# Cross-network kernel: loads of the first rows, bias vectors and first weights on other queues, and the prologue's small matmuls in one tile shape

## The chip, the core and the metric

The kernel runs on one core of a Trainium2 chip. A core has TensorE for matrix products, VectorE, ScalarE and GpSimd for elementwise work, SyncE for issuing transfers, and 16 DMA engines [...]. TensorE reads from SBUF and writes to PSUM, which here is eight banks of 512 fp32 columns in 128 partitions. The metric is device time in microseconds, the median of several runs; lower is better.

## The reference

The computation is a cross network of six layers on a batch of 4096 rows with 416 features:

```python
B, F, D, L = 4096, 26, 16, 6          # 26 * 16 = 416 features
x = x0                                 # (4096, 416), bf16
for l in range(L):
    x = x0 * (x @ ws[l] + bs[l]) + x   # ws (6, 416, 416), bs (6, 416)
```

The kernel rewrites this. With x = x0 * y, each layer is y <- y + x @ W + b. So PSUM accumulates the sums of x @ W over the layers, and the biases enter as running sums over the layers, computed once at the start.

## The kernel before

**Tiling.** The batch is cut into four superblocks of 1024 rows, each of two halves of 512 rows. Features lie along the partitions, in three chunks of 128 (384 features) and a tail of 32. A layer on a superblock is a set of matmuls with 512 moving columns. TensorE is split into four column tiles of 32: each chunk of outputs is four matmuls `128*32`, which run side by side (`tile_mm`, L265 records them). The tail features use row tiles of 32 (L393, L409). After each group, VectorE forms (PSUM + bias sum) * x0 (L537), and ScalarE and GpSimd do the same for the tail.

**The prologue.** Before the first layer can start, TensorE needs three things. The first is the bias sums `cb_sb`, the second the first rows transposed (`x0T_sb`), the third the first weights W0 (`w_sb`). TensorE's program there is, in order:

- 40 warm-up matmuls on a constant (L130), which need no data;
- `bias_sums()`: 16 matmuls of 6 columns, which multiply `bsa_sb` (a row of ones over the six bias rows) with `u_sb` (a triangle of ones);
- `fill(1)`: one round of four more matmuls on the constant;
- twelve transposes (L312) of the first 512 rows, in the order of `IN_ORDER`: three column chunks of the row pair `h = 1`, then three of `h = 0`. VectorE (L512) and ScalarE (L561) copy the results to `x0T_sb`;
- the first layer, n = 0, whose first chunk waits for W0 and for these copies. In its middle stand `tail_inputs()` and `third_input()`, which bring the tail features and the third row pair in feature order by products with the identity matrix.

Rows 768 to 1023 come by a transposing DMA that SyncE issues when the row pair 0 has landed (L158).

**The queues.** SyncE and ScalarE each issue transfers in program order. Row pair i is `xin_sb[:, 2*i:2*i+2, :]`, 208 KB, with semaphore `s_xin[i]`. SyncE issues the biases, pair 0, pair 2. ScalarE issues pair 1, W0 (312 KB), the tail columns of the last rows (`xtl_sb`), two pieces of `wt_sb`, and then begins its computing work, which opens with a load of its activation table. GpSimd issues the rest of layer 0's tail weights and waits for a cleared `wc_sb` first (`s_zero`).

**Semaphores that the change touches.** `s_bs` (biases loaded), `s_zero` (VectorE's memsets done), `s_set` (GpSimd's identity and triangle made), `s_xin[0..2]` (row pairs loaded), `s_w[0]` (W0 loaded), `s_inT` (a chunk transposed), `s_inD` and `s_inA` (copied by VectorE, by ScalarE).

Of the kernel before, what the change touches and what calls it, by code (L numbers as in the profile page):

```python
# [8 lines left out]
ACTF = mybir.ActivationFunctionType  # L9


def bass_standalone__dcn_v2_cross__recsys_kernel(
# [6 lines left out]
    B, D = x0.shape  # L19
    L = ws.shape[0]  # L20
# [7 lines left out]
    G = SB // 4  # L28
# [4 lines left out]
    with ExitStack() as es:  # L33
        def sb(name, shape, dt=BF16):
            return es.enter_context(nc.sbuf_tensor(name, shape, dt))
# [4 lines left out]
        xin_sb = sb("xin_sb", [128, 6, D])  # L40
        xtl_sb = sb("xtl_sb", [128, 2, DR])
        x4_sb = sb("x4_sb", [128, NS - 1, SB])
        x0T_sb = sb("x0T_sb", [128, NC, B])
# [10 lines left out]
        o_sb = sb("o_sb", [128, NJ, D])  # L54
        ident = sb("ident", [128, 128])
        ones_sb = sb("ones_sb", [128, 256])
        bsa_sb = sb("bsa_sb", [L + 1, D])
        u_sb = sb("u_sb", [L + 1, L])
        cb_sb = sb("cb_sb", [128, NC + 1, L], FP32)
        cq_sb = sb("cq_sb", [128, NC + 2], FP32)  # L60
        ps = es.enter_context(nc.psum_tensor("ps", [128, 8, 512], FP32))
        psT = ps.bitcast(BF16)
# [4 lines left out]
        s_ones, s_set, s_zero = sem("s_ones"), sem("s_set"), sem("s_zero")  # L67
        s_wtp, s_wc = sem("s_wtp"), [sem("s_wc%d" % i) for i in range(2)]
        s_bs, s_cbp, s_cb = sem("s_bs"), sem("s_cbp"), sem("s_cb")
        s_xin = [sem("s_xin%d" % i) for i in range(3)]  # L70
# [4 lines left out]
        s_inT, s_inD, s_inA = sem("s_inT"), sem("s_inD"), sem("s_inA")  # L75
# [12 lines left out]
        x0_w = x0.rearrange("(g p r) d -> p g r d", p=128, r=2)  # L88
# [9 lines left out]
        IN_BANKS = ((3, 4, 6), (0, 5, 7))  # L98
        IN_ORDER = ((1, 0), (1, 1), (1, 2), (0, 0), (0, 1), (0, 2))
        THIRD = (3, 6, 7)  # L100
# [4 lines left out]
        def lane(g):  # L105
            return slice(32 * g, 32 * g + 32)
# [22 lines left out]
        for q in range(4 * 10):  # L129
# [1 line left out]
                ps[lane(q % 4), 7, 0:256], lhsT=CONST[:, 0:32], rhs=CONST, start=True, stop=True,  # L131
                skip_group_check=True, tile_position=(0, 32 * (q % 4)),
            )
        nc.sync.dma_start(bsa_sb[1:L + 1, :], bs[:, :]).then_inc(s_bs, 16)
        nc.sync.dma_start(xin_sb[:, 0:2, :], x0_w[:, 0, :, :]).then_inc(s_xin[0], 16)
        nc.sync.dma_start(xin_sb[:, 4:6, :], x0_w[:, 2, :, :]).then_inc(s_xin[2], 16)
        nc.scalar.dma_start(xin_sb[:, 2:4, :], x0_w[:, 1, :, :]).then_inc(s_xin[1], 16)
        nc.scalar.dma_start(w_sb[:, 0, :, :], wmain(0)).then_inc(s_w[0], 16)
        nc.scalar.dma_start(xtl_sb[:, :, :], x0_v[:, 6:JS, DF:D]).then_inc(s_xtl0, 16)
        nc.gpsimd.memset(ones_sb[:, :], 1.0).then_inc(s_ones, 1)  # L140
        nc.vector.memset(wc_sb[:, :, :], 0.0).then_inc(s_zero, 1)
        nc.vector.memset(bsa_sb[0:1, :], 1.0).then_inc(s_zero, 1)

        es2 = ExitStack()
        block = es2.enter_context(nc.Block())
# [56 lines left out]
        @block.gpsimd  # L202
        def _(pool):
            def load_wc(i, g):
                a, b = ((0, 1), (1, L))[i]
                pool.dma_start(
                    wc_sb[lane(g), a:b, 32 * g:32 * g + 32], ws[a:b, DF:D, DF:D].rearrange("l p n -> p l n")
                ).then_inc(s_wc[i], 16)

            pool.wait_ge(s_ones, 1)  # L210
            pool.affine_select(
                out=ident[:, :], in_=ones_sb[:, 0:128], pattern=[[-1, 128]],
                compare_op=ALU.is_equal, fill=0.0, base=0, channel_multiplier=1,
            ).then_inc(s_set, 1)
            pool.affine_select(
                out=u_sb[:, :], in_=ones_sb[0:L + 1, 0:L], pattern=[[1, L]],
                compare_op=ALU.is_ge, fill=0.0, base=1, channel_multiplier=-1,
            ).then_inc(s_set, 1)
            for g in (0, 2):
                load_wt(pool, g, 0, 1, s_wtp)  # L220
            pool.wait_ge(s_zero, 1)
            for i in range(2):
                for g in (1, 3):
                    load_wc(i, g)

            for s in range(NS):
                pool.wait_ge(s_te, s + 1)
                for l in range(L):
                    n = s * L + l + 1
                    if n == NL:  # L230
                        break
                    if n == 1:
                        pool.tensor_scalar(
                            out=cq_sb[:, 0:NC + 1], in0=cb_sb[:, :, L - 1], scalar1=-1.0, scalar2=None, op0=ALU.add
                        ).then_inc(s_cq, 1)
                        pool.wait_ge(s_cq, 1)
                        pool.tensor_tensor(
                            out=cq_sb[:, NC + 1:NC + 2], in0=cq_sb[:, NC:NC + 1], in1=cb_sb[:, NC, L - 2:L - 1], op=ALU.subtract
                        ).then_inc(s_cq, 1)
                    pool.wait_ge(s_ta, n)  # L240
                    dst = xot_sb[:, s, :] if l == L - 1 else xt_sb[:, (l + 1) % 2, 0:G]
                    pool.tensor_tensor(  # L242
                        out=dst, in0=t32_sb[:, n % 2, :], in1=x0t_sb[:, s, 0:G], op=ALU.mult
                    ).then_inc(s_xt, 1)
                    if n == NL - 1:
                        pool.tensor_scalar(
                            out=xot_sb[:, s, :], in0=t32_sb[:, n % 2, :], scalar1=cq_sb[:, NC + 1:NC + 2], scalar2=None, op0=ALU.add
                        ).then_inc(s_qt, 1)
                    if l == 2 and s > 0:
                        pool.wait_ge(s_ot, 16 * s)  # L250
                        pool.tensor_copy(
                            out=o_sb[:, (s - 1) * JS:s * JS, DF:D].rearrange("p (g r) f -> p r g f", r=2),
                            in_=ot_sb[:, s - 1, :, :].rearrange("p r (g f) -> p r g f", f=DR),
                        ).then_inc(s_otc, 1)
            pool.wait_ge(s_x0n, 16)
            for i, t in enumerate(POOL_TILES):
                pool.wait_ge(s_oA, i + 1)
                pool.tensor_tensor(
                    out=o_sb[:, j0 + t, :], in0=a32_sb[:, i, :], in1=x0n_sb[:, t, :], op=ALU.mult
                ).then_inc(s_oP, 1)  # L260

        @block.tensor
        def _(pe):
            def tile_mm(dst, lhsT, rhs, q, start):
                return pe.matmul(  # L265
                    dst, lhsT=lhsT, rhs=rhs, start=start, stop=True,
                    skip_group_check=True, tile_position=(0, 32 * q),
                )

            def fill(n):  # L270
                for i in range(n):
                    for q in range(4):
                        tile_mm(ps[lane(q), 7, 0:256], CONST[:, 0:32], CONST, q, True)
# [10 lines left out]
            def third_input():  # L284
                pe.wait_ge(s_inD, 4)
                for c in range(NC):
                    for j in range(2):
                        for q in range(4):
                            f0 = c * 128 + 32 * q
                            ins = tile_mm(  # L290
                                ps[lane(q), THIRD[c], j * 128:j * 128 + 128], xin_sb[:, 4 + j, f0:f0 + 32], ident[:, :], q, True
                            )
                    ins.then_inc(s_inT, 1)

# [8 lines left out]
                ins.then_inc(s_cbp, 1)  # L303

            bias_sums()
            fill(1)
            pe.wait_ge(s_set, 1)
            for i, (h, c) in enumerate(IN_ORDER):
                if c == 0:
                    pe.wait_ge(s_xin[h], 16)  # L310
                for j in range(2 * h, 2 * h + 2):
                    ins = pe.transpose(  # L312
                        out=psT[:, IN_BANKS[h][c], (j % 2) * 128:(j % 2 + 1) * 128],
                        in_=xin_sb[:, j, c * 128:(c + 1) * 128], identity=ident[:, :],
                    )
                ins.then_inc(s_inT, 1)

            for s in range(NS):
                for l in range(L):
# [3 lines left out]
                    if l == 0:  # L323
                        src, off = x0T_sb, s * SB
                        srct = x0t_sb[:, s, :]
                    else:
                        src, off = xT_sb[:, l % 2], 0
# [71 lines left out]
                    for part in range(2):  # L399
# [16 lines left out]
                        for h in range(2):  # L416
                            g = 2 * h + 1
                            if part == 1:
                                ins = row(g, ps[:, 6 + h, lo], wc_sb[lane(g), l, 32:160], hi, False)
# [84 lines left out]
        def _(dve):  # L504
            dve.wait_ge(s_cbp, 1)
            dve.tensor_copy(
                out=cb_sb[:, :, :], in_=ps[:, 1, 0:8 * (NC + 1)].rearrange("p (c e) -> p c e", e=8)[:, :, 0:L],
            ).then_inc(s_cb, 1)
            for i, (h, c) in enumerate(IN_ORDER):
                if c != 1:  # L510
                    dve.wait_ge(s_inT, i + 1)
                    dve.tensor_copy(  # L512
                        out=x0T_sb[:, c, h * 256:(h + 1) * 256], in_=psT[:, IN_BANKS[h][c], 0:256]
                    ).then_inc(s_inD, 1)
            for c in (0, 2):
                dve.wait_ge(s_inT, 2 * NC + c + 1)
                dve.tensor_copy(out=x0T_sb[:, c, 512:768], in_=ps[:, THIRD[c], 0:G]).then_inc(s_inD, 1)  # L517
            dve.wait_ge(s_cb, 1)
            for s in range(NS):
                for l in range(L):  # L520
# [35 lines left out]
        def _(act):  # L556
# [18 lines left out]
            act.wait_ge(s_tp, 1)  # L575
            act.activation(out=x0t_sb[:, 0, :], in_=ps[:, 5, :], func=ACTF.Copy).then_inc(s_te, 1)
            act.wait_ge(s_inT, 2 * NC + 2)
            act.activation(out=x0T_sb[:, 1, 512:768], in_=ps[:, THIRD[1], 0:G], func=ACTF.Copy).then_inc(s_inA, 1)
            act.wait_ge(s_cb, 1)
            for s in range(NS):  # L580
                for l in range(L):
# [77 lines left out]
```

## Time and profile before

| | us |
|---|---|
| median of 3 runs | 128.12 |
| lowest and highest | 128.09 and 128.29 |
| span of the profiled execution | 127.6 |

The profile shows one execution. Its times are microseconds from the start of the span. A line of the timeline gives the start, the duration, the engine and the source line, then the operation with the tile that it writes and those that it reads, and the count. PE is the matmul side of TensorE and PEld its weight loads; an engine's name with a q at the end is its queue, where transfers are issued. Brackets at the end of a line hold the idle time before it and what ended it. A matmul `128*32 128x512` has 128 rows of weights by 32 columns and 512 moving columns. The end of a matmul is modelled, so starts are the safer thing to compare.

| engine | busy us | share of the span |
|---|---|---|
| TensorE (PE) | 124.1 | 97% |
| VectorE (DVE) | 99.9 | 78% |
| ScalarE (ACT) | 67.7 | 53% |
| GpSimd (POOL) | 24.1 | 19% |

### The profile page before, as it was taken

Reading aid. Unit: us, or ns where it says so; the run is one execution under the profiler, and the core shown is the slowest. Engines: PE = TensorE matmul, PEld = TensorE weight load, DVE = VectorE, ACT = ScalarE, POOL = GpSimd, SP = SyncE. Lnnn points to the kernel's source line nnn. Section 1 sums busy time; section 2 is a strip of 40 time slices with the busy share of each in tenths; the row PEclk is TensorE's granted clock in tenths of the full one; section 3 lists DMA queues with packets and bytes.
Section 4 is the critical chain, followed back from the end, with each engine's and each line's share of the span. In section 5 each row is a group of like instructions: output and inputs, shape, how many; then the busy total and the mean of one; then the engine's idle time right before and its main releaser. Section 6 shows DMA issues by size and latency. Waiting matters only on the chain.

```text
span 127.6 us, 5323 instructions
## 1 busy us (share of the span) xinstructions
PE 124.1 (97%) x2410; PEld 62.6 (49%) x2410; DVE 99.9 (78%) x154; ACT 67.7 (53%) x146; POOL 24.1 (19%) x44
## 2 busy tenths in 40 slices
PE   7999999999999999999999999999999999999991
PEld 5654445445445445445445445444454454454660
DVE  2329779779789788798797797797797797797973
ACT  0626456475735554575753573575762564566830
POOL 7512012012022023022022022021021020220441
DMA  3950799500009959720006899960007920430006
GB/s 114 272 124 13 161 257 231 147 0 0 5 3 91 189 85 251 224 74 5 0 5 118 154 116 234 322 201 0 5 0 46 184 47 0 157 115 5 0 27 246
DMA packets 31889, 13.49 MB, mean 106 GB/s; under 512 B 24950, under 2 KB 31868, under 8 KB 31868
## 3 DMA queue, kind: packets, MB, share of 16 engines
q1 hardware_dynamic: 30476, 12.12, 44.6%
q10 hardware_dynamic: 1200, 0.99, 2.4%
q8 instruction: 19, 0.31, 1.0%
q0 software_dynamic: 192, 0.06, 0.3%
q14 instruction: 2, 0.02, 0.0%
HBM read 3.86 MB, written 3.41 MB: 57 GB/s over the span
## 4 chain that ended last, share of the span: by engine, by line
PE 97%; DVE 0%; issue 0%
PE ps L265 82%; PE ps L393 10%; PE ps L130 2%; PE ps L449 2%; PE ps L312 1%; PE ps L464 1%; DVE o_sb L550 0%; PE ps L488 0%; PE ps L409 0%; PE ps L494 0%
## 5 line engine op out<-in xcount | busy, mean ns | idle before, releaser
L537 DVE SCALAR_TENSOR_TENSOR xT_sb<-ps,cb_sb,x0T_sb 128x512 bf16<-128x512 f32 x120 | 81.0, 744 | 16.4 <-PE ps L393 16.3
L265 PE MATMUL ps<-xT_sb,w_sb 128*32 128x512 bf16 (+1 forms) x1596 | 84.2, 364 | 0.0
L265 PEld LDWEIGHTS ps<-xT_sb,w_sb 128*32 128x32 bf16 x1596 | 40.9, 97 | 37.2 <-issue 4.0
L566 ACT ACTIVATE xt_sb<-xt_sb 32x256 bf16<-32x256 bf16 x76 | 31.5, 414 | 15.8 <-POOL xt_sb L242 15.1
L595 ACT ACTIVATE t_sb<-ps,cb_sb 64x256 f32<-64x256 f32 x46 | 21.6, 469 | 31.1 <-PE ps L265 30.8
L242 POOL TENSOR_TENSOR xt_sb<-t_sb,x0t_sb 128x256 bf16<-128x256 f32 x20 | 13.5, 674 | 81.4 <-ACT t_sb L595 81.4
L265 PE MATMUL ps<-x0T_sb,w_sb 128*32 128x512 bf16 (+1 forms) x336 | 19.2, 375 | 0.0
L537 DVE SCALAR_TENSOR_TENSOR xo_sb<-ps,cb_sb,x0T_sb 128x512 bf16<-128x512 f32 x18 | 12.1, 743 | 2.5 <-PE ps L393 2.5
L265 PEld LDWEIGHTS ps<-x0T_sb,w_sb 128*32 128x32 bf16 x336 | 8.8, 99 | 8.2 <-issue 1.8
L393 PE MATMUL ps<-xt_sb,wt_sb 32*128 32x512 bf16 x76 | 11.5, 379 | 0.0
L614 ACT ACTIVATE x0t_sb<-x_sb 32x512 bf16<-32x512 bf16 x12 | 7.5, 626 | 0.3
L409 PE MATMUL ps<-xt_sb,wt_sb 32*128 32x512 bf16 x38 | 7.4, 385 | 0.0
L393 PE MATMUL ps<-xt_sb,wc_sb 32*128 32x256 bf16 x76 | 7.3, 268 | 0.0
L393 PEld LDWEIGHTS ps<-xt_sb,wt_sb 32*128 32x128 bf16 x76 | 2.2, 92 | 8.1 <-DVE xT_sb L537 8.1
L393 PEld LDWEIGHTS ps<-xt_sb,wc_sb 32*128 32x128 bf16 x76 | 3.8, 93 | 2.2
L242 POOL TENSOR_TENSOR xot_sb<-t_sb,x0t_sb 128x256 bf16<-128x256 f32 x3 | 2.0, 677 | 12.6 <-ACT t_sb L595 12.6
L550 DVE SCALAR_TENSOR_TENSOR o_sb<-ps,x0n_sb 128x416 bf16<-128x416 f32 x6 | 3.3, 585 | 1.0 <-PE ps L494 0.9
L570 ACT ACTIVATE xo_sb<-ps,cq_sb 128x512 bf16<-128x512 f32 x5 | 3.3, 686 | 1.1 <-PE ps L393 1.1
L130 PE MATMUL ps<-const-bfloat16-1.0 128*32 128x256 bf16 x40 | 2.3, 418 | 0.8 <-PEq L644 0.8
L561 ACT ACT_TABLE_LOAD x1 | 1.3, 1283 | 3.2 <-issue 3.2
L517 DVE CAST x0T_sb<-ps 128x256 bf16<-128x256 f32 x2 | 0.8, 419 | 2.6 <-PE ps L265 2.6
L449 PE MATMUL ps<-w_sb,xT_sb 128*128 128x416 bf16 x12 | 2.8, 340 | 0.0
(52 smaller groups left out, 41.9 us busy)
## 6 DMA issues: line engine op xcount, KB each, us to landing
out_dram<-o_sb SPq DMA_DIRECT2D x2, 832.0 KB, 5.0
w_sb<-in_ws_dram SPq DMA_DIRECT2D x5, 312.0 KB, 3.9
x0n_sb<-in_x_dram SPq DMA_DIRECT2D x1, 832.0 KB, 5.4
out_dram<-o_sb SPq DMA_DIRECT2D x1, 624.0 KB, 3.6
out_dram<-o_sb SPq DMA_DIRECT2D x3, 208.0 KB, 2.0
xin_sb<-in_x_dram SPq DMA_DIRECT2D x2, 208.0 KB, 3.2
out_dram<-o_sb ACTq DMA_DIRECT2D x2, 208.0 KB, 2.0
w_sb<-in_ws_dram ACTq DMA_DIRECT2D x1, 312.0 KB, 3.6
```

What stands on the lines that cost most here:

```text
L130: nc.tensor.matmul(ps[lane(q % 4), 7, 0:256], lhsT=CONST[:, 0:32], rhs=CONST, start=True, stop=True, skip_group_check=True, tile_position= ...
L242: pool.tensor_tensor(out=dst, in0=t32_sb[:, n % 2, :], in1=x0t_sb[:, s, 0:G], op=ALU.mult).then_inc(s_xt, 1)
L265: return pe.matmul(dst, lhsT=lhsT, rhs=rhs, start=start, stop=True, skip_group_check=True, tile_position=(0, 32 * q),)
L393: return pe.matmul(dst, lhsT=lhsT, rhs=srct[lane(g), cols], start=l == 0 and start, stop=True, skip_group_check=True, tile_position=(32 * ...
L409: pe.matmul(ps[:, NC * h + 2, :], lhsT=wt_sb[lane(g), l, 0:128], rhs=srct[lane(g), :].rearrange("p (b r) -> p b r", b=2)[:, ::-1, :], star ...
L449: pe.matmul(ps[:, NAT_BANKS[t], 0:D], lhsT=xT_sb[:, (L - 1) % 2, k, rows], rhs=w_sb[:, L - 1, k, :], start=False, stop=True, skip_group_ch ...
L537: dve.scalar_tensor_tensor(out=dst, in0=ps[:, NC * half + c, :], scalar=cb_sb[:, c, l:l + 1], in1=x0T_sb[:, c, o:o + H], op0=ALU.add, op1= ...
L550: dve.scalar_tensor_tensor(out=o_sb[:, j0 + t, :], in0=ps[:, NAT_BANKS[t], 0:D], scalar=1.0, in1=x0n_sb[:, t, :], op0=ALU.add, op1=ALU.mul ...
L566: ins = act.activation(out=buf[lane(g), G:2 * G], in_=buf[lane(g ^ 1), 0:G], func=ACTF.Copy)
L570: act.activation(out=xo_sb[:, NS - 1, c, half * H:(half + 1) * H], in_=ps[:, NC * half + c, :], func=ACTF.Identity, bias=cq_sb[:, c:c + 1] ...
L595: ins = act.activation(out=t32_sb[HALVES[h], n % 2, :], in_=tail(h), func=ACTF.Identity, bias=cb_sb[HALVES[h], NC, l:l + 1],)
L614: ins = act.activation(out=x0t_sb[lane(g), s + 1, :].rearrange("p (b n) -> p b n", b=2), in_=src[:, ::-1, :] if g % 2 else src, func=ACTF. ...
```

## The change

The change reorders the first transfers and gives the prologue's small TensorE work one shape.

- All three row pairs go to SyncE's queue, pair 1 first. The biases go to the head of ScalarE's queue, before W0. They then no longer stand ahead of the rows.
- `bsa_sb` and `u_sb` grow from 7 rows to 128, the unused rows zero. For this VectorE clears the whole of `bsa_sb` before the biases are loaded into it, so ScalarE waits for that memset before it issues the load. The aim is that the bias matmuls have the same tile shape, 128 rows by 32 columns, as the warm-up before and the fill after them.
- The transposes of the first two pairs are done in column tiles of 32 as well, four small ones where there was one of 128 columns. Those of the third pair become transposes, with bf16 results, where they were products with fp32 results.
- The fill behind the bias sums is two rounds long.

```diff
-        bsa_sb = sb("bsa_sb", [L + 1, D])
-        u_sb = sb("u_sb", [L + 1, L])
+        bsa_sb = sb("bsa_sb", [128, D])
+        u_sb = sb("u_sb", [128, L])
...
-        nc.sync.dma_start(bsa_sb[1:L + 1, :], bs[:, :]).then_inc(s_bs, 16)
+        nc.sync.dma_start(xin_sb[:, 2:4, :], x0_w[:, 1, :, :]).then_inc(s_xin[1], 16)
         nc.sync.dma_start(xin_sb[:, 0:2, :], x0_w[:, 0, :, :]).then_inc(s_xin[0], 16)
         nc.sync.dma_start(xin_sb[:, 4:6, :], x0_w[:, 2, :, :]).then_inc(s_xin[2], 16)
-        nc.scalar.dma_start(xin_sb[:, 2:4, :], x0_w[:, 1, :, :]).then_inc(s_xin[1], 16)
+        nc.scalar.wait_ge(s_zero, 1)
+        nc.scalar.dma_start(bsa_sb[1:L + 1, :], bs[:, :]).then_inc(s_bs, 16)
         nc.scalar.dma_start(w_sb[:, 0, :, :], wmain(0)).then_inc(s_w[0], 16)
...
+        nc.vector.memset(bsa_sb[:, :], 0.0).then_inc(s_zero, 1)
+        nc.vector.wait_ge(s_zero, 1)
+        nc.vector.memset(bsa_sb[0:1, :], 1.0).then_inc(s_zero, 1)
         nc.vector.memset(wc_sb[:, :, :], 0.0).then_inc(s_zero, 1)
-        nc.vector.memset(bsa_sb[0:1, :], 1.0).then_inc(s_zero, 1)
...
-                out=u_sb[:, :], in_=ones_sb[0:L + 1, 0:L], pattern=[[1, L]],
+                out=u_sb[:, :], in_=ones_sb[:, 0:L], pattern=[[1, L]],
...
-            pool.wait_ge(s_zero, 1)
+            pool.wait_ge(s_zero, 3)
...
+            def tile_tp(dst, src, q):
+                return pe.transpose(out=dst, in_=src, identity=ident[:, :], tile_position=(0, 32 * q))
...
-                            ins = tile_mm(
-                                ps[lane(q), THIRD[c], j * 128:j * 128 + 128], xin_sb[:, 4 + j, f0:f0 + 32], ident[:, :], q, True
+                            ins = tile_tp(
+                                psT[lane(q), THIRD[c], j * 128:j * 128 + 128], xin_sb[:, 4 + j, f0:f0 + 32], q
                             )
...
             bias_sums()
-            fill(1)
+            fill(2)
...
-                for j in range(2 * h, 2 * h + 2):
-                    ins = pe.transpose(
-                        out=psT[:, IN_BANKS[h][c], (j % 2) * 128:(j % 2 + 1) * 128],
-                        in_=xin_sb[:, j, c * 128:(c + 1) * 128], identity=ident[:, :],
-                    )
+                for j in range(2):
+                    for q in range(4):
+                        f0 = c * 128 + 32 * q
+                        ins = tile_tp(
+                            psT[lane(q), IN_BANKS[h][c], j * 128:j * 128 + 128], xin_sb[:, 2 * h + j, f0:f0 + 32], q
+                        )
...
-                dve.tensor_copy(out=x0T_sb[:, c, 512:768], in_=ps[:, THIRD[c], 0:G]).then_inc(s_inD, 1)
+                dve.tensor_copy(out=x0T_sb[:, c, 512:768], in_=psT[:, THIRD[c], 0:G]).then_inc(s_inD, 1)
...
-            act.activation(out=x0T_sb[:, 1, 512:768], in_=ps[:, THIRD[1], 0:G], func=ACTF.Copy).then_inc(s_inA, 1)
+            act.activation(out=x0T_sb[:, 1, 512:768], in_=psT[:, THIRD[1], 0:G], func=ACTF.Copy).then_inc(s_inA, 1)
```

## The prediction

> **What bounds the kernel now.** I read the page first: the busy shares and the chain that ended last.
>
> ```profile
> PE 124.1 (97%) x2410; PEld 62.6 (49%) x2410; DVE 99.9 (78%) x154; ACT 67.7 (53%) x146; POOL 24.1 (19%) x44
> ```
>
> ```profile
> PE 97%; DVE 0%; issue 0%
> ```
>
> TensorE is busy for 124.1 of 127.6 us and holds 97% of the chain. So the end moves only if TensorE does its work at another pace or if a pause in that work grows or shrinks. The diff touches only the time before the layers run, so the next view is the timeline from 0 to 16 us (columns: start, duration, both in us, engine, line, operation, names, count):
>
> ```profile
> 0.84 2.33 PE L130 MATMUL ps<-const-bfloat16-1.0 128*32 128x256 bf16 x40 [0.84 <-PEq L644]
> 0.97 0.46 DVE L141 MEMSET wc_sb<- 128x480 uint32 x1 [0.97 <-PEq L644]
> ...
> 1.45 0.41 DVE L142 MEMSET bsa_sb<- 1x416 bf16 x1
> ...
> 3.09 0.27 PE L265 MATMUL ps<-u_sb,bsa_sb 7*32 7x6 bf16 x16
> ...
> 3.29 0.40 PE L265 MATMUL ps<-const-bfloat16-1.0 128*32 128x256 bf16 x4
> ...
> 3.63 1.46 PE L312 MATMUL ps<-ident,xin_sb 128*128 128x128 bf16 x12
> ...
> 5.14 2.47 PE L265 MATMUL ps<-x0T_sb,w_sb 128*32 128x512 bf16 x28
> ```
>
> Here is the whole prologue of TensorE: 40 warm-up matmuls, 16 bias matmuls, one round of fill, 12 transposes, then the first layer matmul at 5.14. What follows is nearly gapless, so a later or earlier 5.14 is what the change can buy or lose. The third view is the weight loads of that stage, one line for a group of four column tiles:
>
> ```profile
> 5.11 0.17 PEld L265 LDWEIGHTS ps<-x0T_sb,w_sb 128*32 128x32 bf16 x8 [0.29 <-DMA w_sb<-in_ws_dram]
> 5.52 0.18 PEld L265 LDWEIGHTS ps<-x0T_sb,w_sb 128*32 128x32 bf16 x4 [0.25 <-issue]
> 5.95 0.18 PEld L265 LDWEIGHTS ps<-x0T_sb,w_sb 128*32 128x32 bf16 x4 [0.25 <-issue]
> 6.38 0.18 PEld L265 LDWEIGHTS ps<-x0T_sb,w_sb 128*32 128x32 bf16 x4 [0.25 <-issue]
> 6.79 0.33 PEld L265 LDWEIGHTS ps<-x0T_sb,w_sb 128*32 128x32 bf16 x8 [0.23 <-issue]
> 7.22 0.11 PEld L265 LDWEIGHTS ps<-ident,xin_sb 128*32 128x32 bf16 x3
> ```
>
> The starts lie 0.43 us apart up to 6.38; two groups then fit between 6.79 and 7.22, 0.215 each. TensorE doubles its pace at about 6.8 us, though the page grants it full clock throughout. Some four groups run at half pace, about 0.8 us lost.
>
> The last view is the transfers (size, median us from issue to landing), and one line of it alone:
>
> ```profile
> xin_sb<-in_x_dram SPq DMA_DIRECT2D x2, 208.0 KB, 3.2
> ...
> w_sb<-in_ws_dram ACTq DMA_DIRECT2D x1, 312.0 KB, 3.6
> xin_sb<-in_x_dram ACTq DMA_DIRECT2D x1, 208.0 KB, 2.6
> ```
>
> ```profile
> L135 SPq DMA_DIRECT2D xin_sb<-in_x_dram x1: 369/369/369, 1.3 to 1.3; - x1
> ...
> DMA to landing us min/median/max: 2.7/2.7/2.7
> ```
>
> With the issue times of the timeline (0.81, 1.26, 1.21, 1.68), row pair 1 lands at 3.4, pair 0 at 3.96, W0 at 4.8, pair 2 at 5.4 (its own line answers 3.7). The order alternates ScalarE, SyncE, ScalarE, SyncE, although W0 was issued 0.05 us before pair 0. [...]
>
> [...] the fill at 3.29 streams for about 0.21, yet the first transpose is at 3.63, 0.12 later, with its rows landed at 3.4. Likewise ten rounds of warm-up at 0.213 from 0.84 end at 2.97 and the bias matmuls come at 3.09. So what the view books as a wait for the bias load I read as a drain.
>
> **The change, part by part.**
>
> *Bias vectors.* Their load moves from first on SyncE's queue (issued 0.80) to first on ScalarE's, behind a wait for a new VectorE memset. That memset starts at 0.97 as the old one did. Two rows price it: 480 elements took 0.46, 416 took 0.41. Zeros over 128x416 bf16 fit 208 32-bit words like the wc_sb row, so 0.23 us; if left as bf16, 0.41. I take 0.23, as both are zero fills: it ends at 1.20, and ScalarE issues at about 1.25. Queued behind the wait on ScalarE are the W0 load (1.21 before, now about 1.25 + 0.40 = 1.65), the tail rows, two wt loads, and the activation table load (3.24 before, now about 3.65, ending 4.9). ScalarE's copies of x0T then end at 5.7 where they ended at 5.3. Their reader is the second third of the first chunk, three groups after 5.14, near 6.4: hidden. The page gives no landing for the bias load. The quickest landings elsewhere in the page are 1.9 to 2.0 us after issue, and the first row load took 2.6. From 1.25 that gives 3.15 to 3.85. [...] I take 2.1: 3.35. The bias matmuls then start at 3.35, 0.26 later than now.
>
> *128-row bias sums.* The same 16 matmuls of 6 columns; zero rows add no columns. They took 0.20 to the fill, drain included. Without a change of row tiling I put them at 0.13. The two affine selects gain rows, not columns, and are over at 1.62: hidden.
>
> *Fill of two rounds.* One more group at 0.213.
>
> *Transposes in column tiles.* 48 instead of 12, in groups of four that stream 128 columns. The old twelve start 0.107 apart, which is 128 columns at half pace; 12 groups cost the same. Bounds: 0.107 a group if the four overlap as the identity matmuls of pair 2 do now (40 of them from 7.43 to 7.99, 0.056 a group at full pace), far more if they ran singly. I take 0.107. The drain of 0.12 before them goes. They start at 3.35 + 0.13 + 0.43 = 3.91 against 3.63: 0.28 later. Now it takes 1.51 from the first transpose to the first layer matmul (copies by VectorE included), so that comes at 5.42.
>
> *Rows.* Pair 1 leaves SyncE at the same 0.80; pairs 0 and 2 keep their order. But pair 0 now stands in the same queue as pair 1, and W0, issued at 1.65, alone in the other. The first loads, issued at 0.80, move their first data at about 1.8 (the share of DMA time is zero until then), so W0 could move from about 2.7. Pair 1's packets end on most engines between 2.7 and 3.0. [...] Pair 0 would land when W0 does now, near 4.7 instead of 3.96. From the first transpose of pair 0's column block 0 (3.63 + 6 x 0.107 = 4.27) to 5.14 are 0.87 us, so the layer would start at 4.75 + 0.87 = 5.62: 0.48 later. I think this likelier than not.
>
> *Third row pair.* 24 transposes for 24 matmuls at 0.056 a group: the same. The fp32 casts (419 ns) become bf16 copies (291 ns, as L512 now), 0.13 each saved, but ScalarE's copy of the tail rows, 0.60 from 7.91, ends at 8.51 and is what holds the next step at 8.60. Nothing gained. GpSimd's wait for three memsets ends at about 2.1; it gets there at 2.84: hidden.
>
> *Sum.* The layers start 0.28 to 0.48 later. If the pace still doubles at 6.8, half of it is made good, since groups that move past 6.8 run at 0.215: 0.14 to 0.24. If the doubling moves with the work, 0.28 to 0.48. The middle of the likelier half, 0.36, gives 128.12 + 0.36 = 128.5.
>
> **The rivals.**
>
> *Faster: the pace doubles earlier.* The drains go, the fill is longer [...]. If it doubles by 5.4, four groups save 0.213 each: 128.12 + 0.28 - 0.85 = 127.55; in part, 127.8. [...] Against it: the pause before the bias sums grows from 0.12 to about 0.4.
>
> *No change.* The bias lands at 3.15, W0 comes too late to pass pair 0, and the removed drains pay for the second fill: layers at 5.2, half of it made good, 128.15.
>
> *Much slower.* [...]
>
> **How the numbers follow.** Chances: forecast (0.26 to 0.6 later) 0.45; earlier doubling 0.24; no change 0.23; lost window 0.08. So faster 0.24, same 0.23, slower 0.53. The range runs from 127.5, where the earlier doubling is nearly whole, to 129.3, which takes in a bias load landing at 3.85 (0.5 more) with pair 0 late; the lost window stays outside.
>
> **What would show it.** Right: bias matmuls near 3.35 with fill straight behind, first transposes near 3.9, a pause among the transposes until pair 0 lands near 4.7, layers at 5.4 to 5.65, pace doubling at 6.8 or later. Wrong: layer groups 0.215 us apart before 6.4, pair 0 landed by 4.0, bias sums before 3.2, or any difference arising after 9.2 us.

## The result, and the profile after

The changed kernel takes 132.25 us (median of 4 runs, 131.53 to 133.78), beside 128.20 for the kernel before in the same runs (128.09 to 128.99). The ratio is 1.028, with a 95% interval from 1.021 to 1.036. It is slower, as predicted, but by 4.05 us where I had said 0.4, and far outside my range. Ratios and intervals, here and below, leave out executions more than 1.5% above the fastest of their kernel; the medians keep them.

The page of the changed kernel, in the parts that answer to those shown of before: busy time, the chain that ended last, and the transfers of the rows and of W0.

```profile
PE 124.8 (95%) x2450; PEld 62.8 (48%) x2450; DVE 99.9 (76%) x155; ACT 67.5 (52%) x146; POOL 24.0 (18%) x44
...
PE 92%; DMA 4%; DVE 1%; issue 0%; ACTq 0%
...
xin_sb<-in_x_dram SPq DMA_DIRECT2D x3, 208.0 KB, 2.6
...
w_sb<-in_ws_dram ACTq DMA_DIRECT2D x1, 312.0 KB, 5.8
```

TensorE's work has hardly grown (124.8 against 124.1), but the chain now holds 4% of waiting for a transfer, which it did not before. The last line names it: W0 lands 5.8 us after its issue, where it took 3.6.

The timeline of the changed kernel (start, duration, engine, line, operation, and in brackets the idle time before it with what ended it):

```profile
0.91 0.23 DVE L142 MEMSET bsa_sb<- 128x208 uint32 x1 [0.91 <-PEq L651]
1.18 0.59 ACTq L138 DMA_DIRECT2D bsa_sb<-in_bs_dram  x1
...
1.79 0.42 ACTq L139 DMA_DIRECT2D w_sb<-in_ws_dram  x1
...
3.38 0.28 PE L268 MATMUL ps<-u_sb,bsa_sb 128*32 128x6 bf16 x16 [0.22 <-DMA bsa_sb<-in_bs_dram]
...
3.51 0.60 PE L268 MATMUL ps<-const-bfloat16-1.0 128*32 128x256 bf16 x8
...
3.89 1.50 PE L274 MATMUL ps<-ident,xin_sb 128*32 128x128 bf16 x48
3.91 1.28 SPq L161 DMA_TRANSPOSE x0T_sb<-in_x_dram  x1
...
7.60 0.14 PEld L268 LDWEIGHTS ps<-x0T_sb,w_sb 128*32 128x32 bf16 x8 [2.48 <-DMA w_sb<-in_ws_dram]
7.60 3.06 PE L268 MATMUL ps<-x0T_sb,w_sb 128*32 128x512 bf16 x28 [2.21 <-DMA w_sb<-in_ws_dram]
8.01 0.16 PEld L268 LDWEIGHTS ps<-x0T_sb,w_sb 128*32 128x32 bf16 x4 [0.27 <-issue]
8.43 0.16 PEld L268 LDWEIGHTS ps<-x0T_sb,w_sb 128*32 128x32 bf16 x4 [0.27 <-issue]
...
10.14 0.15 PEld L268 LDWEIGHTS ps<-ident,xin_sb 128*32 128x32 bf16 x3 [0.27 <-issue]
```

Read it in three steps. Down to 3.89 it is the prediction: the memset takes 0.23, the bias sums come at 3.38 and the transposes at 3.89. The transposing load at 3.91 waits for row pair 0 alone, so pair 0 had landed by then. It was not overtaken. Then TensorE stands still from about 5.2 to 7.60 and waits for W0. After that its groups start 0.41 to 0.43 us apart, at half pace, for seven groups.

**Where the microseconds are.** The first tail matmul of the layer, before and after:

```profile
8.60 0.37 PE L393 MATMUL ps<-x0t_sb,wt_sb 32*128 32x512 bf16 x1
11.66 0.37 PE L400 MATMUL ps<-x0t_sb,wt_sb 32*128 32x512 bf16 x1
```

From there the two traces run in step: 11.66 - 8.60 = 3.06 is the whole difference of the spans (130.7 - 127.6 = 3.1). Of it, 7.60 - 5.14 = 2.46 is the later first layer; the rest, 0.60, is about three more groups at half pace (3 x 0.213 = 0.64).

The medians differ by more, 4.05 against the 2.96 between the two profiled executions. Of the rest, 0.77 lies with before, whose profiled execution took 128.97 for a median of 128.20, and 0.32 with after (131.93 for 132.25). The profiled execution of before had four groups at half pace, 4 x 0.213 = 0.85 us. Over all the comparisons of this document the kernel before was run 85 times: 39 runs lie below 128.4 us, 38 between 128.4 and 129.3, and 8 above 130. I infer that the lowest cluster has no groups at half pace. It is not shown, since no run of it was profiled.

### The profile page after: what moved, and what is told of

It is laid out like the page before. It is cut to its first block, busy times and chain, and to the rows that moved or that the text cites. A ratio compares the mean times of both kernels' runs of the same rounds, so it can differ in the third digit from the quotient of the medians.

```text
span 130.7 us, 5404 instructions
## 1 busy us (share of the span) xinstructions
PE 124.8 (95%) x2450; PEld 62.8 (48%) x2450; DVE 99.9 (76%) x155; ACT 67.5 (52%) x146; POOL 24.0 (18%) x44
## 4 chain that ended last, share of the span: by engine, by line
PE 92%; DMA 4%; DVE 1%; issue 0%; ACTq 0%
PE ps L268 80%; PE ps L400 10%; DMA w_sb<-in_ws_dram 4%; PE ps L456 2%; PE ps L471 1%; DVE o_sb L557 0%; PE ps L495 0%; DVE bsa_sb L144 0%; PE ps L274 0%; DVE bsa_sb L142 0%; PE ps L416 0%; ACTq L138 0%; PE ps L501 0%
## 5 line engine op out<-in xcount | busy, mean ns | idle before, releaser
L268 PE MATMUL ps<-x0T_sb,w_sb 128*32 128x512 bf16 (+1 forms) x336 | 19.8, 384 | 2.2 <-DMA w_sb<-in_ws_dram 2.2
L524 DVE COPY x0T_sb<-ps 128x256 bf16<-128x256 bf16 x2 | 0.5, 292 | 5.3 <-PE ps L274 5.3
L245 POOL TENSOR_TENSOR xot_sb<-t_sb,x0t_sb 128x256 bf16<-128x256 f32 x3 | 2.0, 672 | 12.6 <-ACT t_sb L602 12.6
L583 ACT ACTIVATE x0t_sb<-ps 128x512 bf16<-128x512 f32 x1 | 0.6, 597 | 5.3 <-PE ps L268 5.3
```

The lines of the kernel that those rows point to most:

```text
L245: pool.tensor_tensor(out=dst, in0=t32_sb[:, n % 2, :], in1=x0t_sb[:, s, 0:G], op=ALU.mult).then_inc(s_xt, 1)
L268: return pe.matmul(dst, lhsT=lhsT, rhs=rhs, start=start, stop=True, skip_group_check=True, tile_position=(0, 32 * q),)
```

## The experiments

The theory before the runs was that W0's later issue put its packets behind everything else, and that the pause this made then kept TensorE at half pace. The rivals were the TensorE part of the change, the new order of the row pairs, pair 2 ahead of W0 on the same engines, the transposing load of the last rows, and fetching of instructions.

All profiled executions are collected here first. The columns are: W0 issued, W0 complete (the last of its 16 completions in the trace), first layer matmul, first tail matmul, the time between these two, and the time of that execution, all in us.

| kernel | W0 issued | complete | first layer | first tail | between | time |
|---|---|---|---|---|---|---|
| before | 1.21 | 4.80 | 5.14 | 8.60 | 3.46 | 128.97 |
| after | 1.79 | 7.56 | 7.60 | 11.66 | 4.06 | 131.93 |
| e1 TensorE part alone | 1.22 | 5.52 | 5.57 | 8.44 | 2.87 | 128.81 |
| e2 queues alone | 1.41 | 6.50 | 6.55 | 10.50 | 3.95 | 130.78 |
| e3 W0 ahead of the wait | 0.80 | 4.50 | 6.53 | 10.28 | 3.75 | 130.55 |
| e4 pair 2 behind W0 | 1.78 | 6.42 | 6.46 | 10.84 | 4.38 | 131.21 |
| e5 work while W0 loads | 1.79 | 7.16 | 7.64 | 10.33 | 2.69 | 130.69 |
| e6 last rows after W0 | 1.78 | 6.57 | 6.61 | 9.30 | 2.69 | 129.58 |
| e7 more warm-ups | 1.23 | 5.11 | 5.15 | 8.16 | 3.01 | 128.52 |
| e8 fewer warm-ups | 1.78 | 6.96 | 7.00 | 12.04 | 5.04 | 132.64 |
| e9 queues and wait | 1.78 | 6.92 | 6.96 | 11.99 | 5.03 | 132.49 |
| e10 W0 later alone | 1.89 | 6.84 | 6.88 | 11.32 | 4.44 | 131.55 |
| e11 gap filled | 1.23 | 4.83 | 5.21 | 8.55 | 3.34 | 128.84 |

The time less the first tail matmul is 120.2 to 120.4 in every row but e8 and e9 (120.5 to 120.6, where the tail itself still runs at half pace). So every kernel here differs in the prologue and nowhere else, and two numbers carry most of it: when the layer starts, and how much of "between" is over the 2.69 that e5 and e6 need at full pace. Two rows need care. In e1 and e7 no group runs at half pace either; there the third row pair (e1, 6.91) and the tail columns (e7, 6.86) landed late, where before had them at 5.37 and 5.69, and TensorE waited for them.

**e1, the TensorE part alone.** Tiled transposes, third pair as transposes, two rounds of fill; queues, waits and 7-row biases as before.

```diff
-            fill(1)
+            fill(2)
...
-                    ins = pe.transpose(
+                        ins = tile_tp(
```

> TensorE's part of the change alone: transposes in column tiles, bf16 results for the third pair, two rounds of fill; queues and the 7-row biases as before. If the loss comes from the order of the loads, W0 lands near 4.8 us as before, the first layer matmul is within 0.2 us of 5.14 and the time is 127.8 to 128.6 us. If the tiled transposes themselves keep TensorE at half pace, its groups stay 0.43 us apart past 7 us and the time is 129 us or more.

Measured: 128.79 us (20 runs, 128.37 to 129.41) beside 128.21; ratio 1.003, interval 1.002 to 1.005. Its timeline:

```profile
3.69 1.49 PE L271 MATMUL ps<-ident,xin_sb 128*32 128x128 bf16 x48
...
5.57 1.20 PEld L265 LDWEIGHTS ps<-x0T_sb,w_sb 128*32 128x32 bf16 x28 [0.65 <-DMA w_sb<-in_ws_dram]
5.57 1.70 PE L265 MATMUL ps<-x0T_sb,w_sb 128*32 128x512 bf16 x28 [0.38 <-DVE x0T_sb L516]
```

The first layer comes 0.43 later, all 28 matmuls of the seven groups take 1.70 us, and there is no half pace at all. This part costs about half a microsecond (0.58 at the median) and not four. I had expected W0 near 4.8 and the layer within 0.2 us of before: 14 of W0's 16 pieces were there by 5.00, the last two at 5.49 and 5.52.

**e2, the new order of the queues alone.** No memset, no wait, 7-row biases, TensorE as before.

```diff
-        nc.sync.dma_start(bsa_sb[1:L + 1, :], ...)
+        nc.sync.dma_start(xin_sb[:, 2:4, :], ...)
...
-        nc.scalar.dma_start(xin_sb[:, 2:4, :], ...)
+        nc.scalar.dma_start(bsa_sb[1:L + 1, :], ...)
```

> The queue order of the change alone: pairs 1, 0, 2 on SyncE's queue, biases and W0 on ScalarE's, without the wait for a memset and with 7-row biases and TensorE's work as before. If the service order of the two queues makes W0 late, W0 lands after 5.3 us and the time is 129.5 us or more. If the wait for the memset is what delays W0 (issued 1.79 instead of 1.21), W0 is issued near 1.25 here, lands before 5.1 us, and the time is within 0.5 us of before.

Measured: median 130.21 us (20 runs, in two groups: 7 from 128.5 to 129.1 and 13 from 129.5 to 131.1) beside 128.21. The ratio, over the 12 fastest of the 20, is 1.007 with an interval from 1.003 to 1.010; the medians differ by 2.00. The profiled execution is one of the upper group. There 15 of W0's 16 pieces had landed by 5.09, and one came at 6.50:

```profile
6.55 2.95 PE L265 MATMUL ps<-x0T_sb,w_sb 128*32 128x512 bf16 x28 [1.45 <-DMA w_sb<-in_ws_dram]
```

The layers ran at half pace to about 9.3. So the order alone, with W0 issued 0.2 us later, already costs about half of the whole loss at the median. In this trace one straggling piece makes it, and I did not find its cause. The kernel before has runs above 130 too, but only 8 of 85.

**e3, the changed kernel with W0 first on ScalarE's queue,** ahead of the wait and the biases.

```diff
+        nc.scalar.dma_start(w_sb[:, 0, :, :], wmain(0)).then_inc(s_w[0], 16)
         nc.scalar.wait_ge(s_zero, 1)
         nc.scalar.dma_start(bsa_sb[1:L + 1, :], bs[:, :]).then_inc(s_bs, 16)
-        nc.scalar.dma_start(w_sb[:, 0, :, :], wmain(0)).then_inc(s_w[0], 16)
```

> The changed kernel with W0 issued first on ScalarE's queue, ahead of the wait and the biases. Both theories of a late W0 (service order, delayed issue) expect it to land before 4.6 us and the time back at 127.7 to 128.7 us; rows of pair 0 may then land later than 3.9 us, by up to 0.9. If the time stays above 130 us, something other than W0's place makes the loss.

Measured: 130.86 us (4 runs, 130.00 to 131.20), ratio 1.017, interval 1.010 to 1.023: no cure, where I had expected 127.7 to 128.7. Its timeline:

```profile
4.47 0.28 PE L268 MATMUL ps<-u_sb,bsa_sb 128*32 128x6 bf16 x16 [1.31 <-DMA bsa_sb<-in_bs_dram]
...
4.97 1.50 PE L274 MATMUL ps<-ident,xin_sb 128*32 128x128 bf16 x48
5.06 2.66 SPq L161 DMA_TRANSPOSE x0T_sb<-in_x_dram  x1
...
6.53 1.05 PE L268 MATMUL ps<-x0T_sb,w_sb 128*32 128x512 bf16 x8
6.91 0.18 PEld L268 LDWEIGHTS ps<-x0T_sb,w_sb 128*32 128x32 bf16 x4 [0.24 <-issue]
```

W0 is there at 4.50, but now the six bias rows stand behind it and come at 4.42, and pair 0 at 5.05. This is the overtaking that I had predicted for the changed kernel. It happened with W0 issued at 0.80, and not with 1.79. The chain is now the biases and the transposes, so this run does not tell what an early W0 alone is worth.

**e4, pair 2 moved behind W0** on ScalarE's queue, to see whether pair 2 is what holds W0.

```diff
-        nc.sync.dma_start(xin_sb[:, 4:6, :], x0_w[:, 2, :, :]).then_inc(s_xin[2], 16)
...
         nc.scalar.dma_start(w_sb[:, 0, :, :], wmain(0)).then_inc(s_w[0], 16)
+        nc.scalar.dma_start(xin_sb[:, 4:6, :], x0_w[:, 2, :, :]).then_inc(s_xin[2], 16)
```

> The changed kernel with row pair 2 moved behind W0 on ScalarE's queue; the wait and W0's late issue (1.79 us) stay. [...] W0 lands near 4.8 to 5.2 us and the time is 128 to 129 us. If the late issue alone counts, or a collision with the transposing load of the last rows, W0 still lands after 5.5 us and the time stays above 130 us.

Measured: 130.84 us (4 runs, 129.51 to 131.21), ratio 1.015, interval 1.008 to 1.022. W0's first 15 pieces come 1.1 us earlier than after (5.63 against 6.76; the other five kernels with W0 as late have 6.20 to 6.88) and the last at 6.42. Pair 2 is part of it, not all of it: W0 is still 1.6 us later than before.

**e5, the changed kernel with work in the pause.** Six matmuls on the constant, into a bank that the layer overwrites, stand between the transposes and the wait for W0.

```diff
+            for i in range(6):
+                pe.matmul(ps[:, 2, :], lhsT=WIDE[:, 0:128], rhs=WIDE, start=True, stop=True, ...)
```

> The changed kernel with six matmuls of 512 columns on a constant (about 2.6 us at half pace) between the last transpose and the wait for W0, so that TensorE does not stand idle there. [...] its first layer groups start 0.215 us apart and the time falls by 1 us or more, to 130 to 131.2 us, with the layers starting no earlier. If the pace does not depend on work in that stretch, or W0's lateness is all there is, the groups stay 0.43 apart and the time stays near 132.

Measured: 130.23 us (4 runs, 129.83 to 130.69) beside 128.71 of before; ratio 1.011, interval 1.007 to 1.016. Its timeline:

```profile
5.77 1.94 PE L326 MATMUL ps<-const-bfloat16-1.0 128*128 128x512 bf16 x5 [0.33 <-DVE x0T_sb L524]
...
7.64 1.20 PEld L269 LDWEIGHTS ps<-x0T_sb,w_sb 128*32 128x32 bf16 x28 [0.44 <-DMA w_sb<-in_ws_dram]
7.64 1.69 PE L269 MATMUL ps<-x0T_sb,w_sb 128*32 128x512 bf16 x28
```

(The trace lists five of the six.) The layer starts at 7.64, as late as in the changed kernel (7.60), yet all seven groups run at full pace: 2.69 us to the tail instead of 4.06. The median is 2.0 us below the 132.25 of the changed kernel, and the slowest of these four runs is faster than the fastest of its four. So the half pace is a cost of its own, and work in the pause takes it away: 1.37 us between these two traces. The layer could have started earlier here: W0 was complete at 7.16, and TensorE was still busy with the six matmuls until the layer began.

**e6, the last rows' transposing load held back until W0 has landed.**

```diff
             sp.wait_ge(s_xin[0], 16)
+            sp.wait_ge(s_w[0], 16)
             sp.dma_start_transpose(
```

> The changed kernel with the transposing load of rows 768 to 1023 (L161) issued only when W0 has landed. If those small packets hold up W0's tail, W0 lands before 6.3 us and the time falls by 1 us or more. If W0 is late because of its place in the queues and slow reads before 5.3 us, it lands about as late as in the changed kernel for most DMA engines and the time stays within 0.5 us of 132, or rises where the last rows are then late themselves.

Measured: 131.37 us (4 runs, 129.58 to 131.58), ratio 1.017, interval 1.008 to 1.026. W0 is complete at 6.57, 1.0 earlier than after. In the changed kernel 256-byte packets of the transposing load took up to 1.48 us each between 6.1 and 7.6, just while W0's last pieces were due. So this load may take some of the time. One trace does not show it: of those that leave the load in place, e5 has W0 complete at 7.16 and e8, e9 and e10 have it at 6.84 to 6.96. The profiled run had no half pace and is the fastest of the four; the other three lie 1.7 to 2.0 above it.

```profile
6.61 1.69 PE L269 MATMUL ps<-x0T_sb,w_sb 128*32 128x512 bf16 x28 [1.45 <-DMA w_sb<-in_ws_dram]
```

Set beside the line of e2: the same pause of 1.45 us, and the 28 matmuls take 1.69 here and 2.95 there. A pause does not bring half pace every time.

**e7 and e8, instruction fetches.** The trace shows one 16384-byte packet on the queue that the page calls q8 instruction, which takes 0.95 us, at 8.25 before and at 5.81 after. The theory was that the 36 further transposes and 4 further fill matmuls, 80 instructions with their weight loads, bring it forward. e7 gives the kernel before twice as many warm-ups of half the length (first diff), e8 gives the changed kernel five long ones for its forty (second diff).

```diff
-        for q in range(4 * 10):
+        for q in range(4 * 20):
...
```

```diff
-        for q in range(4 * 10):
+        for q in range(5):
...
```

> The kernel before with its 40 warm-up matmuls of 256 columns cut into 80 of 128 columns: the same columns and loads, 80 more TensorE instructions, as the change adds. If the number of instructions brings the 16 KB instruction fetch forward, it moves from 8.25 us to between 4.5 and 6 us, the transposing load of the last rows lands later than 7.9 us, and the time rises by 0.3 to 1 us. If the fetch does no harm, the time stays within 0.3 us of before.

> The changed kernel with five warm-up matmuls of 128x128 by 512 columns in place of 40 of 128x32 by 256: about the same columns per column tile, 70 fewer TensorE instructions, so that the instruction fetch should fall back to after 7.5 us. If the fetch at 5.81 us is part of what delays W0's last pieces, W0 lands by 6.8 us and the time falls by 0.5 to 1.5 us. If W0 is late by its place in the queues alone, the time stays within 0.5 us of 132.

Measured: e7 128.72 us (20 runs) beside 128.71, ratio 1.001, interval 0.999 to 1.002. The fetch moved to 4.96, and W0 came at 5.11 for 4.80. The tail columns came at 6.86 for 5.69 and held TensorE for about 0.3 us in this trace, yet the median lost nothing. e8 130.92 us (4 runs, 129.89 to 132.64), ratio 1.015, interval 1.007 to 1.023; the fetch moved to 9.18, and W0 was complete at 6.96 for 7.56. At most the fetch accounts for the last 0.6 us of W0's landing, and not for the two before. That much fits the other traces: with the fetch after 8.5 W0 is complete at 6.84 to 6.96 (e8, e9, e10), with the fetch before 6 and the same loads at 7.16 and 7.56 (e5, after). Five traces do not settle it. The spread of e8 is too wide to call its time a gain.

**e9, the changed loads with the TensorE part put back.** 128-row biases, memset, wait and new queues stay.

```diff
-            fill(2)
+            fill(1)
...
-                        ins = tile_tp(
+                    ins = pe.transpose(
```

> The changed kernel with TensorE's part put back: whole transposes, fp32 products for the third pair, one round of fill. Left are the new queues, the memset, the wait and the 128-row biases. If the loads alone make the loss, W0 (issued near 1.8) lands after 6 us, the reads between 3.5 and 4.5 us are slow as in the changed kernel (under 200 GB/s), and the time is 131 to 132.5 us. If the tiled transposes and their instructions are needed for it, the time stays near that of the queues alone, 130.2 us, or below.

Measured: 132.01 us (4 runs, 130.03 to 132.75), ratio 1.017, interval 1.010 to 1.025. The loads alone make most of the loss: 3.42 us over the 128.59 of before, which with the 0.58 of e1 gives 4.00 of the 4.05. W0 is complete at 6.92. The profiled execution is one of the slowest of its kernel, so it is read for the landing and not for the time.

**e10, the kernel before with W0 issued later, and nothing else changed.**

```diff
+        nc.scalar.wait_ge(s_zero, 2)
         nc.scalar.dma_start(w_sb[:, 0, :, :], wmain(0)).then_inc(s_w[0], 16)
```

> The kernel before with one wait added: ScalarE issues W0 when both old memsets are done, near 1.9 us instead of 1.21; everything else as before. If issuing W0 after row pair 2 is what throws it to the end of the loads, it lands after 5.3 us, the reads between 3.5 and 4.5 us are slow as in the changed kernel, and the time is 129.5 us or more. If the new queue order is needed, W0 lands at most 0.7 us later than before, near 5.2 to 5.5 us, without slow reads, and the time is 128.3 to 129 us.

Measured: 131.43 us (4 runs, 131.15 to 132.55) beside 128.59; ratio 1.024, interval 1.018 to 1.030. Its timeline:

```profile
1.89 0.39 ACTq L139 DMA_DIRECT2D w_sb<-in_ws_dram  x1
...
6.88 3.18 PE L266 MATMUL ps<-x0T_sb,w_sb 128*32 128x512 bf16 x28 [1.79 <-DMA w_sb<-in_ws_dram]
7.29 0.16 PEld L266 LDWEIGHTS ps<-x0T_sb,w_sb 128*32 128x32 bf16 x4 [0.27 <-issue]
7.71 0.16 PEld L266 LDWEIGHTS ps<-x0T_sb,w_sb 128*32 128x32 bf16 x4 [0.27 <-issue]
```

This is the clearest run. Old queues, old biases, old transposes: 0.68 us on W0's issue make its landing 2.04 later (6.84 for 4.80) and, with the half pace, a time 2.8 us longer, where the whole change costs 4.05. The interval reaches into that of the whole change. Its 2.8 and the 2.0 of e2 are not parts to be added: each run makes W0 late in its own way. (The wait also puts back what stands behind W0 on ScalarE, 16 KB of tails, two small weight pieces and the table load, by about 0.6.)

What a late W0 meets is seen in the transfers. The windows 3.5 to 4.0 and 4.0 to 4.5 us of three kernels (the last two columns are the time of the packets that begin in the stretch, as a share of the time of 16 engines, which can pass 1, and the GB/s moved), before:

```profile
3.50:4.00 0.50, 0.50 (x8) 0.38 (x5) 0.12 (x1) 0.50 (x1) 0.50 (x2) 1.00 1.12 381
4.00:4.50 0.50, 0.50 (x8) 0.50 (x6) 0.30 (x2) 0.50 (x1) 0.50 (x2) 1.00 1.06 383
```

after:

```profile
3.50:4.00 0.50, 0.50 (x29) 0.40 (x29) 0.18 (x1) 0.24 (x1) 0.50 (x2) 1.00 1.03 92
4.00:4.50 0.50, 0.50 (x28) 0.50 (x24) 0.13 (x1) 0.50 (x1) 0.50 (x2) 1.00 0.67 157
```

and e10:

```profile
3.50:4.00 0.50, 0.50 (x8) 0.38 (x5) 0.12 (x1) 0.15 (x1) 0.50 (x2) 1.00 0.49 127
4.00:4.50 0.50, 0.50 (x8) 0.50 (x6) 0.31 (x2) 0.50 (x1) 0.50 (x2) 1.00 0.90 230
```

After, the packets that begin from 3.5 to 4.0 take nearly as long in all as before (1.03 against 1.12), but there are 34 of them instead of 229, and they move a quarter as much: each takes longer. In the packet records, a 1664-byte row packet that begins in that half microsecond takes 69 ns on average before (3 packets) and 328 after (23). In e10 it is 104 ns and the share is only 0.49, so there it is mostly that less is under way. In the whole microsecond before starts 321 of W0's 384 packets, after 39, e10 57. The kernels divide cleanly by the rate: from 3.5 to 4.0, all seven with W0 issued at 1.78 or later move 72 to 160 GB/s, and all six with W0 issued at 1.41 or earlier move 339 to 381. In part this only says again that W0 is not yet flowing, for in the fast kernels most of these bytes are W0's. But W0's first packets begin at 3.13 to 3.90 in the late kernels and at 3.23 to 3.32 in e1, e2, e7 and e11: they start little later, and then the flow does not build up.

**e11, the kernel before with a round of fill in front of the first layer,** to see whether its own half pace can be had for less.

```diff
+            for q in range(4):
+                tile_mm(ps[lane(q), 2, 0:256], CONST[:, 0:32], CONST, q, True)
```

> The kernel before with one more round of four warm-up matmuls (0.21 us at half pace) between its last transpose and the first layer matmul, where TensorE stands idle for about 0.26 us. [...] runs with a slow start become rarer: the median falls to 128.1 us or stays there, with fewer runs above 128.6. If it does not, the time is the same or up to 0.2 us longer.

Measured: 128.66 us (14 runs) beside 128.59, ratio 1.000, interval 0.998 to 1.003. Nothing is gained. No version here beats the kernel before.

## Why the prediction was wrong

*The direction and the start of the prologue: right.* "Slower" came true, but in good part by luck: of the causes that I gave for it, TensorE's part is worth 0.6 us (e1), and the overtaking of pair 0 did not happen. The memset took the 0.23 that I had priced. The bias sums came at 3.38 (predicted 3.35), the fill stood straight behind them, the transposes came at 3.89 (predicted 3.91) and 48 of them took 1.50 us, 0.107 for a group of four. e1 confirms that the gap of 0.12 before the transposes, which I called a drain, is gone: the fill starts at 3.29, and the tiled transposes follow its two rounds of 0.213 at 3.69. The third pair's shorter copies brought nothing, as said: from its first product or transpose to the first tail matmul are 1.17 us with the old form at full pace (e7) and with the new (e6). GpSimd's longer wait did no harm: its next loads are issued at 2.84 before and after.

*The step that failed: "Rows".* I wrote that W0, "issued at 1.65", "could move from about 2.7", that pair 0 would land late for it, and that the layer would start at 5.62, when pair 0 had come. How the DMA engines share their time between two queues was not shown: the four landings of before (3.4, 3.96, 4.8, 5.4) give an order and no rule. The layer started at 7.60, and the transfer that held it was W0 itself. Three terms went wrong in a row:

- The issue. The bias load holds ScalarE's queue for 0.59 us, where I had put 0.40, so W0 left at 1.79.
- The time from issue to the first packet. I took about 1.0 from the first loads (issued 0.80, moving at 1.8). W0's own first packet in the trace of before came at 2.86, 1.65 after its issue, and I did not look; in other traces it took 1.35 (e4) to 2.1. After, none of its 384 packets begins before 3.5, and by then all packets of pairs 1 and 0 had begun; so nothing was overtaken.
- The landing. This is the largest. The sum has no term for when W0 is complete; it has pair 0 land "when W0 does now". Before, W0 is complete at 4.80 and the layer starts at 5.14, so W0 had 0.34 us to spare. Put off by its issue alone, 0.58, it would have come at 5.38, before my 5.62. From 3.5 to 4.5 it moved 39 packets instead of 321, and it was complete at 7.56. In e10 the later issue alone makes the landing 2.04 later, where the whole change makes it 2.76 later. The fetch and the transposing load (e8, e6) fit the rest, each on few traces: issued at 1.78 or 1.79, W0 is complete anywhere from 6.42 (e4) to 7.56 (after).

*The pace: the rival that I left outside the range.* I had given "lost window", the case in which pauses of 0.4 and 0.5 us keep TensorE longer at half pace, a chance of 0.08; what such pauses cost, no trace had shown. The pause was 2.2, and the doubling came between 10.1 and 10.5, where before had it at 6.8. It comes near 8.9 in e3, 9.3 in e2 and 12.4 in e8 and e9. e5 shows that filling the pause takes the half pace away, worth 1.4 us between the traces and 2.0 between the medians. Even so that rival fell short, because it had no later W0 in it. The two come as a pair: the later W0 makes the pause (2.21 us after, 1.79 in e10), and the pause can cost again.

*A base that was off.* I set the 0.8 us of half pace in the profile of before against the median of 128.12. The profiled run was 128.97. If the runs near 128.1 have no half pace, as I infer above, the median that I started from had none left to lose, and my "faster" rival at 127.55 was hardly to be had.

*What stays open.* Why reads crawl from 3.5 to 4.0 us (72 to 160 GB/s) in the seven kernels with W0 issued at 1.78 or later is not shown. The third layer's weights, nearly alone on the engines in the trace of before, also start slowly (about 60 to 150 ns a packet from 12.6 to 13.2 us, then 40), while W0 beside pair 0 starts at 39. So a slow first stretch of a load, hidden only where others are in full flow, would fit. No run tests it, and none separates it from the later small loads behind W0. The straggling piece of e2 and the half pace that follows one pause and not another (e2, e6) are open too.

## What to carry to other kernels

A load that gates the first compute should be issued ahead of anything small that has to wait: in e10, 0.68 us at the issue came back as 2.04 at the landing. Then see what stands behind it: with W0 first in the changed kernel, the biases came too late instead (4.42 us, e3). Take a load's issue-to-first-packet time from its own packets (1.65 us for W0 before) and not from the first load of the program (1.0). Price a pause on TensorE twice, as the pause itself (2.21 us after) and as the half-pace matmuls that may follow it (1.37 between after and e5), and ask for both whether the profiled run is a typical one. Spare work in the pause gave back the second cost in e5 (2.69 us to the tail for 4.06) and not the first (the layer at 7.64 for 7.60), and it must not outlast the wait.

## What the runs showed of the hardware

- The half pace after a pause differs from trace to trace. In e6, the layers are at full pace from 6.61 after a pause of 1.45 us, in e10 at half pace to about 10.6 after one of 1.79, and in e2 to about 9.3 after the same 1.45. That it also differs between runs of one kernel is inferred from the clusters of their times. The granted clock is 1.00 in both stretches of the changed kernel (7.6 to 10.4 at half pace, 10.4 to 12.0 at full pace), so it doesn't show this.
- A transpose in column tiles runs at the pace of the other matmuls: 0.107 us for a group of four with 128 columns at half pace (after), 0.056 at full pace (third row pair of e6).
- An instruction fetch of 16 KB took 0.94 to 1.51 us. In these runs it came earlier with more TensorE instructions in the prologue: 8.25 before, 5.03 in e1 and 4.96 in e7 with 80 more; 5.81 after, 9.18 in e8 with 70 fewer. In e1 and e7 single pieces of the loads at that time came more than a microsecond after their other pieces (6.86 to 7.14); that they lay on the engine of the fetch is not shown.
- Six rows of 832 bytes cost ScalarE's queue 0.59 us to issue, more than the 312 KB of W0 (0.42). On SyncE's queue, before, they cost 0.40.
